# Rewriting the opening of a Fourier-mixing and gated feed-forward kernel: load queues, matrix phases, the DRAM round trip and the order of the other loads

## The chip, the cores and the metric

The kernel runs on one core of one Trainium2 chip. The metric is the device time of one execution in microseconds; the median of three runs is compared. A core has a matrix engine (TensorE, PE in the profile; PEld is its weight load), three engines for elementwise work (VectorE or DVE, ScalarE or ACT, GpSimd or POOL) and SyncE (SP), which here only issues transfers. SP, ACT and POOL each feed a transfer queue of their own: q1, q10 and q0 in the profile. The 16 DMA engines serve all three.

## The reference: what is computed

For x of shape (8, 3008, 256), in float32:

```python
X = np.fft.fft(np.fft.fft(x, axis=1), axis=2).real      # then rows (24064, 256)
g = X @ w_gate                                          # (256, 1536)
val = X @ w_val
gelu = 0.5 * g * (1.0 + erf(g / sqrt(2)))
out = (gelu * val) @ w_out                              # (1536, 256)
```

## The kernel before: how the work is staged

The sequence length is 3008 = 64 x 47. The Fourier transform over it is done as two matrix stages, and the transform over the 256 channels is folded into the weights.

**Opening.** For batch 0, `load_x` (L157) brings x(0) in three pieces of 8 slots; each piece is two transfers of 64 partitions (h = 0 to partitions 0 to 63, h = 1 to 64 to 127), all on SP's queue. `fold_x` (L172) adds and subtracts mirrored channels (L188, L189) and copies two columns (L190). The matrix G of the first stage is generated: `gen_g` (L246) multiplies and adds phases (L250, L253), reduces them (`reduce_phase`, L243 and L244) and takes a sine on ACT (L256). `a_step` (L396) multiplies G with the folded x, two slots a step, twelve steps a batch; the result is evacuated to S1 by DVE (L402) or ACT (L401) in turn. `z_write` (L405) stores S1 to a DRAM tensor z in two halves of four transfers each (L413, 32 partitions each), and `z_read` (L417, issue L423) reads it back to Ap in two transfers with another partition order: this is the round trip. Meanwhile `gen_t` (L261) and `gen_c` (L292) generate the other matrices, and `gen_w` (L306) casts the two weight matrices from float32 on POOL (L311), multiplies them with the channel matrix CW (L316) and evacuates the products to WE, WOP and WOM (L320 to L323). `load_w` (L209) loads these weights on ACT's queue, `load_wo` (L216, issue L220) the output weights on POOL's queue, casting them on the way; `load_x(1, i)` loads batch 1. `b_steps` (L425) is the second stage: for four q, an even and an odd half of 8 or 16 small matmuls (L442, L443, L448) on Ap, evacuated to Y by DVE (L463). `n_first` (L343) sends one row of Y through DRAM to all partitions (nrow, nq).

**Main loop.** 288 units follow, 36 a batch: three chunks of Y's columns by twelve blocks of the hidden width. A unit has five or six matmuls with 512 columns (`layer1`, L508), two Gelu on ACT (L529, L540), and the products on DVE (L544, L553, and for most units L519 and L558) and POOL (L567). The second layer of the chunk before (L592) is put between, 8 matmuls a unit. The first and second stage of the next batch are spread over the units: `a_step(b + 1, k)` in units 0 to 11 (for batch 1 two a unit, in units 6 to 11), `z_read` in units 12 and 13, `b_steps` later. Loads for batch b + 2 go out at units 0, 12 and 24, their folds on POOL from the fourth unit after.

**What sets the order.** A scheduler lays out each engine's instructions by their readiness in its own model. `keep_in_program_order` (`pin`, L151) ties an instruction behind the one traced before it on its engine. Before, this is on only in the main loop (`held`), and never for SP's transfers. `issue_after(ins)` ties what the block traces on the engine of `ins` behind `ins`: issue order on that engine, nothing else. Before, `load_w` is tied behind an evacuation on ACT, `load_wo` behind a cast on POOL, `load_x(1, i)` behind the last `z_read` on SP (L648). A tile from a pool with `bufs=3`, such as xin, waits until the work on the tile three before it is done.

Of the kernel before, what the change touches and what calls it, by code (L numbers as in the profile page):

```python
# [14 lines left out]
MAGIC = 12582912.0  # L15
TWO_PI = 2.0 * math.pi

# [11 lines left out]
def kernel(  # L29
# [20 lines left out]
    nc = tc.nc  # L50

# [40 lines left out]
    col_a = const_pool.tile([128, 1], FP32)  # L92
    col_b = const_pool.tile([128, 1], FP32)
# [51 lines left out]
    def z_tile():  # L145
        return dram.tile([2, NJ, NG, C], BF16, tag="z", bufs=2, name="z")


    held = [False]

    def pin(ins):  # L151
        return tc.keep_in_program_order(ins) if held[0] else ins
# [4 lines left out]
    def load_x(b, i):  # L157
# [3 lines left out]
        for h in range(2):  # L161
# [6 lines left out]
            nc.sync.dma_start(  # L168
# [3 lines left out]
    def fold_x(b, i, eng, a0=0, an=None):  # L172
# [7 lines left out]
        for (p0, pn, s0, sn) in parts:  # L180
# [7 lines left out]
            pin(eng.tensor_tensor(ea, lo, hi, op=ALU.add))  # L188
            pin(eng.tensor_tensor(od, lo, hi, op=ALU.subtract))  # L189
            pin(eng.tensor_copy(  # L190
# [5 lines left out]
    def iota(t, pattern, base, mult):  # L196
        nc.gpsimd.iota(t, pattern=pattern, base=base, channel_multiplier=mult,
                       allow_small_or_imprecise_dtypes=True)

    iota(col_p, [[0, 1]], 0, 1)  # L200
    iota(rowj, [[15, HJ]], 0, 0)
    iota(_sub(rowk, [[1, 33]], 0), [[1, 33]], 0, 0)
    iota(_sub(rowk, [[1, 31]], 33), [[1, 31]], 1, 0)
    for i in range(3):
        load_x(0, i)
# [3 lines left out]
    def load_w():  # L209
        for i, w_hbm in enumerate((moe_w_gate, moe_w_val)):  # L210
            t = work.tile([128, NCH, F], FP32, tag="h", bufs=2, name="wst")
            wst[i] = t
            src = ap_replace(w_hbm, ap=[[F, 128], [128 * F, NCH], [1, F]], offset=w_hbm.offset)
            nc.scalar.dma_start(out=_sub(t, [[F, NCH], [1, F]], 0), in_=src)

    def load_wo():  # L216
# [3 lines left out]
        nc.gpsimd.dma_start(out=_sub(Wo_sb, [[C, NFC], [1, C]], 0), in_=src)  # L220

    iota(_sub(rowc, [[1, 128]], 0), [[1, 128]], 0, 0)
    iota(_sub(rowc, [[1, 128]], 128), [[1, 128]], 0, 0)
# [5 lines left out]
    def scratch(n, name):  # L229
        return work.tile([128, n], FP32, tag="ev", bufs=3, name=name)  # L230

    xf_zero = [_sub(t, [[1, C]], (HJ - 1) * C, N1, N1) for t in xf_bufs]
    for t in xf_zero:
        nc.vector.memset(t, 0.0)
    nc.vector.memset(G, 0.0)
    nc.vector.memset(_sub(rowq, [[1, 33]], 0), 0.25)
    nc.vector.memset(_sub(rowq, [[1, 31]], 33), 0.0)
    nc.vector.tensor_scalar(col_a, col_p, 64.0, 296.0, op0=ALU.is_ge, op1=ALU.mult)
# [535 lines left out]
```

## Time and profile before

| what | us |
|---|---|
| median of 3 runs (672.79 to 678.3) | 674.6 |
| the profiled execution | 674.43 |
| its span, first to last instruction | 672.7 |
| PE busy, share of the span | 632.1, 94% |
| DVE, ACT, POOL busy | 540.3, 449.9, 460.3 |
| first matmul of stage one (L396) | 13.70 |
| first and second read of z landed (PE goes on) | 41.25 and 44.78 |
| first matmul of the main loop (L508) | 47.33 |
| first matmul of the second layer (L592) | 71.50 |

Times within the execution count from the span's start. A timeline line has start, duration, engine, line, operation, output and inputs, and in brackets the idle time before it and what ended it. A line of the chain has start, duration and the work on it. A line of the windows has each engine's busy time with its instruction count, then the granted clock of PE, the busy share of the DMA engines and their GB/s. A queue line has packets, megabytes, and the time of these packets as a share of 16 engines.

### The profile page before, as it was taken

To read this page: it belongs to the slowest core of one execution; us is meant where nothing else is said; L and a number is where in the kernel's file an instruction comes from. 1 tells how busy PE (TensorE), PEld (TensorE's weight loads), DVE (VectorE), ACT (ScalarE), POOL (GpSimd) and SP (SyncE) were. 2 spreads that over 40 slices of the span, in tenths; PEclk is the share of its full clock that TensorE was granted. 3 is DMA by queue.
4 is the path that set the end of the run, shared out by engine and by line. 5 is a ranking of instruction groups with operands and counts; after the bars stand their busy time and mean duration, and the time that the engine had idled before them with its cause. 6 is when DMAs were issued, how large, how long until landed. Compare 5 with 4: busy or idle time off the path is not lost.

```text
span 672.7 us, 13986 instructions
## 1 busy us (share of the span) xinstructions
PE 632.1 (94%) x4571; PEld 414.4 (62%) x4624; DVE 540.3 (80%) x896; ACT 449.9 (67%) x944; POOL 460.3 (68%) x726
## 2 busy tenths in 40 slices
PE   1389999998999999999999999999999999999997
PEld 0144666665666666666666666666666666666666
DVE  7947988696877978788886987778886998789981
ACT  2347667775777767776677776786777767666662
POOL 1409698886698886977788886977778444645450
PEclk9989999998999999999999999999999999999999
DMA  8898854557457465357453574266221463111113
GB/s 183 282 232 179 195 147 106 126 124 196 103 130 164 119 159 131 80 133 177 109 131 92 125 183 119 69 152 157 76 62 44 97 168 74 45 33 46 48 48 76
DMA packets 65577, 82.70 MB, mean 123 GB/s; under 512 B 8959, under 2 KB 59359, under 8 KB 61408
## 3 DMA queue, kind: packets, MB, share of 16 engines
q1 hardware_dynamic: 63408, 77.87, 48.1%
q10 hardware_dynamic: 544, 3.15, 1.4%
q0 software_dynamic: 1552, 0.79, 0.9%
q8 instruction: 36, 0.59, 0.4%
q14 instruction: 37, 0.30, 0.2%
HBM read 45.13 MB, written 37.44 MB: 123 GB/s over the span
## 4 chain that ended last, share of the span: by engine, by line
PE 87%; DMA 5%; DVE 5%; issue 1%; ACT 1%; SPq 0%; ACTq 0%; DVEq 0%
PE ps_o L592 36%; PE ps_g L508 25%; PE ps_v L508 19%; DMA Ap<-z 4%; PE ps_d L396 2%; PE ps_d L448 2%; DMA xin<-in_x_dram 1%; DVE h L544 1%; DVE h L553 1%; DVE xf L189 1%; DMA z<-S 0%; DVE S L402 0%; DVE ev L519 0%; DVE xf L188 0%; DVE sc L244 0%
## 5 line engine op out<-in xcount | busy, mean ns | idle before, releaser
L567 POOL TENSOR_TENSOR h<-gl,dv 128x512 bf16<-128x512 bf16 (+1 forms) x216 | 246.6, 1142 | 152.3 <-DVE dv L558 110.4
L592 PE MATMUL ps_o<-Wo_sb,h 128*128 128x256 bf16 (+2 forms) x2304 | 297.5, 273 | 0.0
L544 DVE TENSOR_TENSOR h<-gl,ps_v 128x512 bf16<-128x512 bf16 (+1 forms) x288 | 192.2, 677 | 99.3 <-ACT gl L540 77.1
L529 ACT ACTIVATE gl<-ps_g 128x512 bf16<-128x512 f32 (+1 forms) x288 | 169.4, 588 | 151.8 <-PE ps_g L508 110.2
L592 PEld LDWEIGHTS <-h 128*128 128x128 bf16 (+2 forms) x2304 | 227.4, 100 | 66.4 <-issue 2.5
L540 ACT ACTIVATE gl<-ps_g 128x512 bf16<-128x512 f32 (+1 forms) x288 | 168.7, 586 | 6.8 <-remote 6.3
L519 DVE SCALAR_TENSOR_TENSOR ev<-nq,WN,ps_v 128x512 f32<-128x512 bf16 (+1 forms) x216 | 157.6, 730 | 4.2 <-PE ps_v L508 2.7
L558 DVE SCALAR_TENSOR_TENSOR dv<-ev,ps_v 128x512 f32<-128x512 f32 (+1 forms) x216 | 144.2, 668 | 0.0
L508 PE MATMUL ps_v<-Y,WE 128*128 128x512 bf16 (+1 forms) x287 | 108.3, 378 | 1.0 <-DVE h L553 0.4
L508 PE MATMUL ps_g<-Y,WOM 128*128 128x512 bf16 (+1 forms) x288 | 108.0, 375 | 0.1
L508 PE MATMUL ps_g<-Y,WOP 128*128 128x512 bf16 (+1 forms) x281 | 105.5, 376 | 2.0
L508 PE MATMUL ps_v<-Y,WOP 128*128 128x512 bf16 (+1 forms) x281 | 105.7, 376 | 0.4
L508 PE MATMUL ps_g<-Y,WE 128*128 128x512 bf16 (+1 forms) x250 | 93.9, 376 | 0.0
L188 POOL TENSOR_TENSOR xf<-xin 128x127 bf16<-128x127 f32 (+3 forms) x148 | 72.4, 489 | 23.6 <-DMA xin<-in_x_dram 22.0
L508 PEld LDWEIGHTS <-WOP 128*128 128x128 bf16 x576 | 56.0, 97 | 48.5 <-issue 2.9
L189 POOL TENSOR_TENSOR xf<-xin 128x127 bf16<-128x127 f32 (+3 forms) x148 | 72.5, 490 | 0.0
L508 PEld LDWEIGHTS <-WE 128*128 128x128 bf16 x576 | 56.3, 98 | 26.0 <-issue 1.8
L603 ACT ACTIVATE osb<-ps_o 128x512 f32<-128x512 f32 x80 | 47.8, 597 | 26.6 <-PE ps_o L592 23.9
L448 PEld LDWEIGHTS <-Ap 96*128 96x128 bf16 (+1 forms) x527 | 40.5, 97 | 32.0 <-issue 7.0
L553 DVE TENSOR_TENSOR h<-gl,ps_v 128x512 bf16<-128x512 bf16 (+1 forms) x72 | 48.5, 673 | 2.5 <-PE ps_v L508 2.3
L401 ACT ACTIVATE S<-ps_d 128x512 bf16<-128x512 f32 x74 | 44.7, 604 | 1.3 <-PE ps_d L396 1.3
L508 PEld LDWEIGHTS <-WOM 128*128 128x128 bf16 x360 | 35.1, 97 | 16.9 <-issue 1.1
(103 smaller groups left out, 379.8 us busy)
## 6 DMA issues: line engine op xcount, KB each, us to landing
out_dram<-osb SPq DMA_DIRECT2D x360, 64.0 KB
xin<-in_x_dram SPq DMA_DIRECT2D x40, 512.0 KB
z<-S SPq DMA_DIRECT2D x64, 192.0 KB
Ap<-z SPq DMA_DIRECT2D x16, 768.0 KB
xin<-in_x_dram SPq DMA_DIRECT2D x8, 448.0 KB
ngr<-nrow SPq DMA_DIRECT2D x7, 388.0 KB
wst<-in_moe_w_gate_dram ACTq DMA_DIRECT2D x1, 1536.0 KB
wst<-in_moe_w_val_dram ACTq DMA_DIRECT2D x1, 1536.0 KB
```

What stands on the lines that cost most here:

```text
L188: pin(eng.tensor_tensor(ea, lo, hi, op=ALU.add))
L189: pin(eng.tensor_tensor(od, lo, hi, op=ALU.subtract))
L448: pin(nc.tensor.matmul(ps[r, o : o + N2], w, t[:, s : s + N2], start=True, stop=True))
L508: pin(nc.tensor.matmul(ps[:, :n], W[:, i, r["fs"]], r["Y"][:, eo, r["c0"] : r["c0"] + n], start=start, stop=True, skip_group_check=not start))
L519: pin(nc.vector.scalar_tensor_tensor(r["ev"][:, :nm], r["nq"][:, r["c0"] : r["c0"] + nm], WN[:, fc : fc + 1], r["pv"][:, :nm], op0=ALU.mul ...
L529: pin(nc.scalar.activation(r["glm"][:, : r["nm"]], r["pg"][:, : r["nm"]], AF.Gelu))
L540: pin(nc.scalar.activation(r["glp"][:, :n], r["pg"][:, :n], AF.Gelu))
L544: pin(nc.vector.tensor_tensor(r["h"][:, r["fc"], :n], r["glp"][:, :n], r["pv"][:, :n], op=ALU.mult))
L553: pin(nc.vector.tensor_tensor(hm, r["glm"][:, :nm], pv[:, :nm], op=ALU.mult))
L558: pin(nc.vector.scalar_tensor_tensor(dv[:, :nm], r["ev"][:, :nm], 2.0, pv[:, :nm], op0=ALU.mult, op1=ALU.subtract))
L567: pin(nc.gpsimd.tensor_tensor(hm, r["glm"][:, :nm], r["dv"][:, :nm], op=ALU.mult))
L592: pin(nc.tensor.matmul(ps[:M, s * C : (s + 1) * C], h[:, fc, sign * 512 + sub * 128 : sign * 512 + sub * 128 + M], Wo_sb[:, fc, :], start= ...
```

## The change: what it does

- Every engine's instructions are tied in program order from the start (`_InOrder`); `pin` and `held` go. On SP only the transfers of batch 0 are tied (`sync`); the others keep `nc.sync`.
- x(0) goes out with h = 0 on SP's queue and h = 1 on ACT's.
- The phases of G (rowj x rowk + rowq) are computed on POOL, three times two operations of 128x512; DVE keeps the reduction. The offsets of rowj come from the iotas.
- `gen_c`'s DVE part goes ahead of `gen_g`; its sines (`sin_c`) come after the last `a_step`. `gen_t` is rewritten for the new partition order, its sines (`sin_t`) lie between parts of `gen_w`.
- z becomes [24, 128, 256], slot by slot. `z_write` is one transfer of 128 partitions; batch 0 writes three pieces of 8 slots and reads slots 0 to 15 (64 partitions of Ap) after the second piece and slots 16 to 23 (32 partitions) after the third. Later batches write two pieces and read as before.
- Pieces of 8 slots: fold of x(0) on DVE, with the last 2 or 3 slots of the second and third piece on POOL; four `a_step`, eight of the twelve evacuations on ACT only.
- The weights come in three column blocks of 512, the first behind x(0) on ACT's queue, the others after the first and second `z_write`; `gen_w` runs by block. The casts become [128, 2, 512].
- `load_x(1, i)` stands after the second stage, under `issue_after` of its first matmul (on PE). x(1)'s fold leaves the opening: 12 parts of two slots in units 1 to 8, on POOL and DVE in turn, at the end of a unit. `load_wo` goes to unit 1, `gen_tw` to unit 13; x(2)'s first load to unit 4.
- Batch 0's second stage takes four PSUM tags instead of two, its odd halves are evacuated on ACT, and a Gelu ahead of it brings the activation table in.

The diff, cut to its core:

```diff
+class _InOrder:
+    def __init__(self, tc, engine):
+        self._tc, self._engine = tc, engine
+
+    def __getattr__(self, name):
+        call = getattr(self._engine, name)
+        return lambda *a, **k: self._tc.keep_in_program_order(call(*a, **k))
...
+    sync, vec, act, pool, pe = (
+        _InOrder(tc, e) for e in (nc.sync, nc.vector, nc.scalar, nc.gpsimd, nc.tensor))
...
-        return dram.tile([2, NJ, NG, C], BF16, tag="z", bufs=2, name="z")
-
-
-    held = [False]
-
-    def pin(ins):
-        return tc.keep_in_program_order(ins) if held[0] else ins
+        return dram.tile([HJ, 128, C], BF16, tag="z", bufs=2, name="z")
...
-            nc.sync.dma_start(
+            eng = act if h and b == 0 else sync if b == 0 else nc.sync
+            eng.dma_start(
...
+    for i in range(3):
+        load_x(0, i)
+    for h in range(2):
+        iota(_sub(rowj, [[1, HJ]], 0, h * N1, N1), [[15, HJ]], 360 * h, 1)
     iota(col_p, [[0, 1]], 0, 1)
...
+    pool.tensor_scalar(rowk, rowk, 1.0 / 64.0, None, op0=ALU.mult)
+    pool.memset(_sub(rowq, [[1, 33]], 0), 0.25)
+    pool.memset(_sub(rowq, [[1, 31]], 33), 0.0)
...
-    def load_w():
+    def load_w(f0):
         for i, w_hbm in enumerate((moe_w_gate, moe_w_val)):
-            t = work.tile([128, NCH, F], FP32, tag="h", bufs=2, name="wst")
-            wst[i] = t
-            src = ap_replace(w_hbm, ap=[[F, 128], [128 * F, NCH], [1, F]], offset=w_hbm.offset)
-            nc.scalar.dma_start(out=_sub(t, [[F, NCH], [1, F]], 0), in_=src)
+            if i not in wst:
+                wst[i] = work.tile([128, NCH, F], FP32, tag="h", bufs=2, name="wst")
+            src = ap_replace(
+                w_hbm, ap=[[F, 128], [128 * F, NCH], [1, 512]], offset=w_hbm.offset + f0)
+            act.dma_start(out=_sub(wst[i], [[F, NCH], [1, 512]], f0), in_=src)
...
+    load_w(0)
+
+    def scratch(n, name):
+        return work.tile([128, n], FP32, tag="ev", bufs=3, name=name)
+
+    PH = []
+    for j0 in range(0, HJ, 8):
+        ph = scratch(512, "sa")
+        PH.append(ph)
+        v = _sub(ph, [[64, 8], [1, 64]], 0)
+        pool.tensor_tensor(
+            v, _sub(rowj, [[1, 8], [0, 64]], j0), _sub(rowk, [[0, 8], [1, 64]], 0), op=ALU.mult)
+        pool.tensor_tensor(v, v, _sub(rowq, [[0, 8], [1, 64]], 0), op=ALU.add)
...
+    vec.memset(xf_zero[0], 0.0)
+    vec.memset(G, 0.0)
+
+    def reduce_phase(ph, tmp):
+        vec.tensor_scalar(tmp, ph, MAGIC, None, op0=ALU.add)
+        vec.scalar_tensor_tensor(tmp, tmp, MAGIC, ph, op0=ALU.subtract, op1=ALU.subtract)
...
+    def gen_g(i):
+        red = red_tile()
+        reduce_phase(PH[i][:, :], red[:, :])
...
+        reds = []
         for t in range(NCH):
-            nc.vector.tensor_scalar(col_c, col_p, 128.0 * t, 1.0 / C, op0=ALU.add, op1=ALU.mult)
-            ph, tmp, red = scratch(512, "sa"), scratch(512, "sb"), scratch(512, "sc")
-            f = lambda u: u[:, :C]
-            nc.vector.scalar_tensor_tensor(f(ph), rowc, col_c, quac, op0=ALU.mult, op1=ALU.add)
-            reduce_phase(f(ph), f(tmp), f(red))
-            nc.scalar.activation(
-                _sub(CW, [[1, C]], t * C), f(red), AF.Sin, scale=-TWO_PI)
-
-
-    def gen_w():
-        nc.vector.tensor_scalar(col_m, col_p, 1.0, -2.0, op0=ALU.is_ge, op1=ALU.mult)
+            vec.tensor_scalar(col_c, col_p, 128.0 * t, 1.0 / C, op0=ALU.add, op1=ALU.mult)
+            both = red2_tile()
+            ph, red = both[:, :C], both[:, C : 2 * C]
+            vec.scalar_tensor_tensor(ph, rowc, col_c, quac, op0=ALU.mult, op1=ALU.add)
+            reduce_phase(ph, red)
+            reds.append(red)
+        vec.tensor_scalar(col_m, col_p, 1.0, -2.0, op0=ALU.is_ge, op1=ALU.mult)
+        return reds
...
+    def sin_c(reds):
+        for t in range(NCH):
+            act.activation(_sub(CW, [[1, C]], t * C), reds[t], AF.Sin, scale=-TWO_PI)
+
+    wbs = []
...
+            pool.tensor_copy(wb[:, :, fs], wst[i][:, :, fs])
...
-        if k % 2 or b > 1:
-            return pin(nc.scalar.activation(dst, ps, AF.Copy))
-        return pin(nc.vector.tensor_copy(dst, ps))
+        if b > 1 or (k % 2 if b else k < 8 or k % 2):
+            return (act.activation(dst, ps, AF.Copy))
+        return (vec.tensor_copy(dst, ps))
...
+        dst = ap_replace(
+            z[0:1, 0, :], ap=[[C, 128], [128 * C, nj], [1, C]], offset=z[j0, 0:1, :].offset)
+        (nc.sync if b else sync).dma_start(out=dst, in_=_sub(S1, [[C, nj], [1, C]], j0 * C))
...
+    def z_read(b, g0, ng, j0=0, nj=HJ):
         if "Ap" not in st[b]:
             st[b]["Ap"] = Ap_tile()
         z, Ap = st[b]["z"], st[b]["Ap"]
         src = ap_replace(
-            z[0, 0, 0:1, :], ap=[[NG * C, 2 * NJ], [1, ng * C]], offset=z[0, 0, g0 : g0 + 1, :].offset)
-        return nc.sync.dma_start(out=_sub(Ap, [[1, ng * C]], g0 * C), in_=src)
+            z[0:1, 0, :], ap=[[NG * C, 4 * nj], [1, ng * C]], offset=z[j0, g0 : g0 + 1, :].offset)
+        (nc.sync if b else sync).dma_start(
+            out=_sub(Ap, [[1, ng * C]], g0 * C, 4 * j0, 4 * nj), in_=src)
...
-                    box["ps"] = ps_o() if b == 0 and eo else ps_d()
+                    box["ps"] = ((ps_v, ps_o)[q % 2] if eo else (ps_d, ps_g)[q % 2])() \
+                        if b == 0 else ps_d()
...
-                if b:
-                    pin(nc.scalar.activation(o, i, AF.Copy))
+                if b or eo:
+                    (act.activation(o, i, AF.Copy))
                 else:
-                    nc.vector.tensor_copy(o, i)
+                    (vec.tensor_copy(o, i))
...
-    gen_g(0, 8)
-    fold_x(0, 0, nc.vector)
-    gen_g(8, 8)
-    fold_x(0, 1, nc.vector)
-    gen_g(16, 8)
-    fold_x(0, 2, nc.vector)
-    for k in range(12):
-        evac = a_step(0, k)
-        if k == 1:
-            with tc.issue_after(evac.ins):
-                load_w()
-        if k % 6 == 5:
-            z_write(0, 2 * (k - 5), 12)
-    gen_t()
-    gen_c()
-    with tc.issue_after(st[0]["mm"].ins):
-        gen_w()
-    with tc.issue_after(wst["last"].ins):
-        load_wo()
-    for i in range(2):
-        last_read = z_read(0, 16 * i, 16)
-    with tc.issue_after(last_read.ins):
-        for i in range(3):
-            load_x(1, i)
+    reds = gen_c()
     for i in range(3):
-        fold_x(1, i, nc.gpsimd)
-    gen_tw()
+        gen_g(i)
+        nd = (8, 6, 5)[i]
+        fold_x(0, i, vec, 0, nd)
+        if nd < 8:
+            fold_x(0, i, pool, nd, 8 - nd)
+        for k in range(4 * i, 4 * i + 4):
+            a_step(0, k)
+        z_write(0, 8 * i, 8)
+        if i < 2:
+            load_w(512 * (i + 1))
+        if i == 1:
+            z_read(0, 0, NG, 0, 16)
+    z_read(0, 0, NG, 16, 8)
+    sin_c(reds)
+    phase_t = gen_t()
+    vec.memset(xf_zero[1], 0.0)
+    gen_w(0)
+    sin_t(*phase_t)
+    gen_w(512)
+    gen_w(1024)
+    gen_wn()
+    act.activation(col_f[:, :], col_p[:, :], AF.Gelu)
     for q in range(4):
         for eo in range(2):
             steps, evac = b_steps(0, eo, q)
@@ -658,6 +687,9 @@
                 s()
             evac()
     n_first(0)
+    with tc.issue_after(st[0]["bmm"].ins):
+        for i in range(3):
+            load_x(1, i)
...
-            if i % 12 == 0 and b + 2 < B:
+            if i in ((0, 12, 24) if b else (4, 12, 24)) and b + 2 < B:
...
-            if i % 12 >= 4 and b + 2 < B:
-                fold_x(b + 2, i // 12, nc.gpsimd, i % 12 - 4, 1)
+            if b == 0:
+                for k in {1: (0, 1), 2: (2,), 3: (3, 4), 4: (5,), 5: (6, 7), 6: (8,),
+                          7: (9, 10), 8: (11,)}.get(i, ()):
+                    fold_x(1, k // 4, (pool, vec)[k % 2], k % 4 * 2, 2)
+                if i == 1:
+                    load_wo()
+                if i == 13:
+                    gen_tw()
+            f, fp = i % 12 - 4, i // 12
+            if b == 0 and i < 16:
+                f, fp = i - 8, 0
+            if f >= 0 and b + 2 < B:
+                fold_x(b + 2, fp, pool, f, 1)
```

## The prediction, made before the changed kernel ran

> **What bounds the kernel now.** I read the page first: its head and the forty slices of PE.
>
> ```profile
> span 672.7 us, 13986 instructions
> PE 632.1 (94%) x4571; PEld 414.4 (62%) x4624; DVE 540.3 (80%) x896; ACT 449.9 (67%) x944; POOL 460.3 (68%) x726
> PE   1389999998999999999999999999999999999997
> ```
>
> PE is the bound from the third slice on; the first three (50 us) are the opening. The change can win back at most what PE idles there, and what the first units lose. So I read, next, the chain of waits between 20 and 50 us.
>
> ```profile
> 29.46 3.19 DMA z<-S
> 33.11 11.63 DMA Ap<-z
> 44.78 0.37 PE ps_d L448 x8
> ...
> 47.33 1.10 PE ps_v L508 x2
> ```
>
> The round trip ends last: 11.63 us of reading z, then 2.55 us to the first unit. Why the read is slow is told by the queues and the windows.
>
> ```profile
> q0 software_dynamic: 939, 0.48, 91.9%
> q1 hardware_dynamic: 55, 0.45, 35.4%
> ...
> 4.00:6.00 2.00, 0.00 (x0) 0.00 (x0) 0.73 (x2) 0.00 (x0) 0.00 (x0) 1.00 1.04 238
> 18.00:20.00 2.00, 1.28 (x7) 0.61 (x4) 2.00 (x7) 0.00 (x0) 0.00 (x0) 1.00 0.93 369
> ```
>
> From 34 to 38 us the output weights (q0) hold the engines and the read (q1) moves 0.45 MB. From 42 to 46 both queues move 136 packets: one packet each in turn, large or small. A load into 64 partitions runs at 221 to 238 GB/s (x(0), 4 to 6 us), one into 128 at 369 (weights, 18 to 20 us). The last view is DVE beside POOL in the timeline.
>
> ```profile
> 26.86 0.48 DVE L300 SCALAR_TENSOR_TENSOR sa<-rowc,col_c,quac 128x256 f32<-128x256 f32 x1
> 28.09 3.22 POOL L311 CAST wb<-wst 128x1536 bf16<-128x1536 f32 x2 [2.81 <-DMA wst<-in_moe_w_val_dram]
> 28.41 1.57 DVE L244 SCALAR_TENSOR_TENSOR sc<-sb,sa 128x256 f32<-128x256 f32 x1
> 30.01 1.57 DVE L300 SCALAR_TENSOR_TENSOR sa<-rowc,col_c,quac 128x256 f32<-128x256 f32 x1
> ```
>
> The same L300 takes 0.48 us alone and 1.57 beside a cast on POOL: each of the two operations ends just after a cast does. The engines take turns, one operation each, where DVE reads only SBUF. In the main loop DVE reads PSUM and this doesn't show.
>
> **The change part by part.** The sum is made against the profiled execution, 674.43 us (span 672.7 and 1.7 around it), 0.2 below the median of 674.6.
>
> *First fold.* DVE: memsets to 2.84 as now and 0.35; `gen_c` two times 0.48 + 0.28 + 0.45 and 0.4 of small ones; reduction 0.42 + 0.68; fold 1.21 + 1.14 + 0.2. In all 3.2 + 6.4 = 9.6 us if nothing blocks. POOL: seven iotas of 0.13, 0.4 of small ones, then six operations of 512 float32. POOL's fold rows (1016 in 2.34 us) give 1.17 each, 7.0 in all, from 2.2 us. These lie exactly beside `gen_c`. If they alternate with DVE, DVE gets all 7.0 on top, less the 1 us before it arrives, and about 1.4 of POOL's part of the next fold: 17.0. The ends are 9.6 and 17.0; the near row is the pair at 28.41 and 30.01, so I take 17.0. Now this fold ends at 11.6 and the first matmul starts at 13.70. That row shows a cast on POOL, not an operation with two inputs. The Trainium skill (SBUF — State Buffer, two separate sides) says that a VectorE operation with two SBUF inputs and any GpSimd operation that reads SBUF exclude each other for the whole instruction. By that rule 17.0 stands; by its opposite 9.6 would.
>
> *x(0) on two queues.* Six issues of 0.68 on SP become three, and three of 0.43 on ACT. At 229 GB/s piece 0 is there at 8.2 us as now, at 369 about 6.3. With the fold waiting for the reduction until 13.4, both cost nothing. The skill's same page (Can I just issue two DMAs to hit both halves?) says that it is no use, +6%; in the sum that changes nothing, in the fast rival below 1 to 2 us.
>
> *To the last evacuation.* Four steps a piece, evacuated on ACT, 0.53 apart: 17.0 + 0.5 + 2.2 = 19.7. Then ACT issues two weight loads (0.9), runs two sines (1.3) and four evacuations: 24.6. The third fold on DVE has four casts on POOL beside it (1024 at 0.95 ns, 1.0 each) and ends at 28.4; last evacuation 31.0, or 29.0 without the casts. Now 25.5.
>
> *Round trip.* The write of piece 1 goes out at 24.7 against 2.1 MB of weights on the other queue, packet by packet: landed between 27.5 (alone) and 31.7 (weights first). Then SP issues the read of 16 slots: 1.05 MB into 64 partitions at 229 is 4.6 us, with issue and landing 34.5 to 38.6. The third write is queued behind that read on SP and in the ring: 0.52 MB at 310 (z writes now, 26 to 30 us), 36.2 to 40.3. The last read, 0.52 MB at 229: 40.6 to 45.0. Now 44.78. So taking the output weights away is worth about 4 us here, and the later S1 and the added order give it back.
>
> *Weight products.* They begin after `sin_c`, 31.9. 24 matmuls at 0.43 as now (0.22 after some 8 us of work, as at 38.5 now), then 0.8: 41.7. They don't end after the latest read, but nearly.
>
> *Second stage.* All four q lie behind the last read; now half are done by then. Two q take 2.10 us now (44.78 to 46.88); with four PSUM tags I take 0.85 each, with 0.7 for the last evacuation 4.1. First unit: 44.7 to 49.1. The weight products and the reads both point to the upper half; I take 48.0, against 47.33: **+0.7**.
>
> *First units.* x(1)'s fold was POOL's alone (15 us from 49.9, waited for by nobody). Now DVE takes six parts of two slots: the line through 1016 in 1.21 and 127 in 0.27 gives 0.41, twice, and 0.15: 0.97 each, 5.8 in all. Behind it on DVE stand the products of the next unit, for which PE waits two units later. DVE's idle time from 52 to 64 us is 2.1, with the half-clocked stretch from 48 on 5.3. So +0.4 to +3.7; beside POOL's own parts (0.6 an operation) up to 3.5 more; if x(1) isn't there at unit 1, up to 4 more. Queued straight after the last read, its first MB lands at 44.1 + 4.6 + 0.9 = 49.6, before unit 1 ends, so I leave the last two out: **+3.5**.
>
> *Rest.* The output weights, 1536 packets, need 6.5 us alone (235 a us, 34 to 38 us now). They are wanted 24 us after the first unit: covered, unless q1 is full all that time (34 packets a us): up to +3. The write of z for later batches is two issues instead of eight; PE waits for these reads 3.1 us in all:
>
> ```profile
> PE ps_d L442 <- DMA Ap<-z: 3.1, 2, 2.2
> ```
>
> With the slower stretch behind the longer wait 0 to 3.5 us could go; late there is SP's queue more than the write, so **-1**. Program order on all engines is what the main loop had already: 0. The Gelu table (1.28 us) now comes under the last read: 0, or 1.3 if the read is early.
>
> Sum: 674.4 + 0.7 + 3.5 - 1.0 = 677.6, say 678, no change that a measurement of this kernel (about 1%) can tell. Its own range, by the ends above, is 669 to 687.
>
> **The rivals.**
>
> *A, the opening really gets short (faster).* If DVE isn't blocked on POOL, the fold ends at 9.6, the last evacuation at 21.6, the last read lands between 33 and 37.4, weight products at 32.4, first unit at 37 to 41.6, middle 39.3: -8. With the folds in DVE's idle time (+0.4) and -1: 666. For it: x(0) could be twice as fast; the iotas, seen so far, block nobody. Against it: the row of 1.57.
>
> *B, x(1) isn't held (slower).* `issue_after` names a matmul on PE and x(1)'s loads are SP's, so nothing ties them. That SP's loads pass earlier ones is seen:
>
> ```profile
> 54.79 0.47 SPq L168 DMA_DIRECT2D xin<-in_x_dram  x1
> 58.10 0.36 SPq L346 DMA_DIRECT2D nq<-nrow  x1
> ```
>
> The load for batch 2 stands after nq in the program and before it in the queue. Each half piece (0.52 MB) in front of the round trip costs 2.3 us at 229 GB/s. One or two fit into the ring's pauses before the second write. From the third on the first unit moves: three +4, all six +10, of which the wait for x(1) gives 2 back. 678 + 8 = 686. Against it: the load of x(2) at unit 12 (75.03 us) wasn't drawn ahead although its tile was free at about 60.
>
> *C, the output weights late.* q1 full with x(1), x(2) and z until unit 12: +3 on the forecast, 681.
>
> **How the numbers follow.** Chances: forecast 0.42, A 0.30, B 0.20, C 0.08. Faster by over 1% (below 667.9): 0.24 of A and 0.02 of the forecast, 0.26. Slower by over 1% (above 681.3): B's 0.20, 0.09 of the forecast, 0.03 of C: 0.32. Within 1%: 0.42. The range leaves out A's lower end (a first unit before 37) and B with C together: 662 to 688.
>
> **What would show it.** Right: DVE operations of `gen_c` at 1 us and more beside POOL's phases, the first L396 near 17 us, the last read landing at 41 to 45, the first L508 near 48, DVE without idle time in units 1 to 8. Wrong in A's way: `gen_c` at 0.3 to 0.5 us each, first L508 before 42. Wrong in B's way: loads of x(1) between the writes of z on SP's queue, the last read after 48. Wrong in size: a first unit as forecast, but the first L592 more than 30 us after it.

## The result and the profile after

The changed kernel takes 692.97 us (median of four, 690.98 to 698.29), the kernel before 674.86 in the same comparison (672.79 to 678.3): a ratio of 1.0275, 95% interval 1.0204 to 1.0347. It is slower by 18 us, and 693 lies outside the predicted 662 to 688. The profiled execution took 693.31 us, its span is 691.5, 18.8 more than before. Three stretches of PE's work divide that difference:

| stretch | before | after | forecast | measured |
|---|---|---|---|---|
| start to the first matmul of the main loop | 47.3 | 56.9 | +0.7 | +9.5 |
| first 12 units, to the first matmul of the second layer | 24.2 | 26.5 | +3.5 | +2.3 |
| the rest, to the end of the span | 601.2 | 608.2 | -1.0 | +7.0 |

Helpers record nearly every instruction now, so in the profile after nearly all lines are L25 (`_InOrder`), and one reads by tiles. Only SP's untied transfers keep their own: L176 is `load_x`, L443 the z write and L451 the z read of later batches, L604 a store. The head of the page and PE's slices come first; PE and its granted clock are two rows of the same forty slices of 17.3 us.

```profile
span 691.5 us, 13974 instructions
PE   1609899998999989999999999999999999999997
PEclk9957999999999999999999999999999999999999
```

PE's third digit is 0 where it was 8: from 35 to 52 us PE does next to nothing, and its clock falls to 0.5. The windows of the changed kernel (busy time with instruction counts for PE, PEld, DVE, ACT and POOL; clock, DMA share, GB/s):

```profile
40.00:50.00 10.00, 0.00 (x0) 0.00 (x0) 0.00 (x0) 0.00 (x0) 0.00 (x0) 0.50 1.14 221
```

From 40 to 50 us no engine does anything; the DMA engines alone are full. What they carry is told by SP's queue (start, time, engine, line, operation; issues only):

```profile
15.01 1.11 SPq L176 DMA_DIRECT2D xin<-in_x_dram  x2
17.75 0.41 SPq L25 DMA_DIRECT2D z<-S  x1
18.98 0.47 SPq L176 DMA_DIRECT2D xin<-in_x_dram  x1
21.94 0.37 SPq L25 DMA_DIRECT2D z<-S  x1
23.13 1.14 SPq L176 DMA_DIRECT2D xin<-in_x_dram  x1
33.33 0.45 SPq L25 DMA_DIRECT2D Ap<-z  x1
33.89 0.53 SPq L25 DMA_DIRECT2D z<-S  x1
34.47 0.84 SPq L176 DMA_DIRECT2D xin<-in_x_dram  x1
```

The three L176 lines up to 23.13 are four transfers of x(1), four half pieces ahead of the first read of z. The code puts x(1) under `issue_after` of a matmul on PE, and on SP that ties nothing. The first read is issued at 33.33, 11.4 us after the second write, whose landing it waits for. The third write has a half piece of x(1) behind it and a neighbour on POOL's queue. The chain's longest piece puts a price on it (start, time, work), and the queues from 41 to 45 us name the neighbour (packets, MB, share):

```profile
33.89 13.21 DMA z<-S
```

```profile
q0 software_dynamic: 821, 0.42, 75.7%
q1 hardware_dynamic: 818, 0.41, 51.9%
```

q0 is the load of the output weights. POOL, which waits for nothing of x(1) since x(1) is already there, ran ahead to unit 1 of its own program and issued it at 32.42 (31.25 before). So neither of the "other loads" is held back. q0 and q1 move a packet each in turn, and the third write takes 13.2 us.

For the rest of the span, the waits of PE for z:

```profile
PE ps_d L25 <- DMA Ap<-z: 8.0, 4, 3.1
```

3.1 us in two waits before, 8.0 in four now. The first of them, in SP's queue of the changed kernel:

```profile
159.19 0.47 SPq L176 DMA_DIRECT2D xin<-in_x_dram  x1
159.76 0.53 SPq L443 DMA_DIRECT2D z<-S  x1
167.13 0.79 SPq L451 DMA_DIRECT2D Ap<-z  x2
```

A half piece of x stands ahead of the second z write of the batch. It waits for a buffer that POOL's fold frees at 159.2; the write waits behind it on SP, and then behind its 0.5 MB on the engines. By the count of transfers it is the first half of x(4): x(3) ended with its piece of 448 KB at 138.75. In the program it stands 25 units later, so the scheduler drew it ahead by most of a batch. The same stands ahead of the second write in the next three batches (240.76, 321.59 and 399.89), and these are the four waits. Before, the half piece that lay here (the second piece of x(3)) stood behind the write, though still ahead of the reads:

```profile
146.81 2.41 SPq L413 DMA_DIRECT2D z<-S  x4
152.95 0.47 SPq L168 DMA_DIRECT2D xin<-in_x_dram  x1
153.59 0.93 SPq L423 DMA_DIRECT2D Ap<-z  x2
```

### The profile page after: what moved, and what is told of

Its sections match the earlier page's. It is cut to its first block, busy times and chain, and to the rows that moved or that the text cites. A ratio compares the mean times of both kernels' runs of the same rounds, so it can differ in the third digit from the quotient of the medians.

```text
span 691.5 us, 13974 instructions
## 1 busy us (share of the span) xinstructions
PE 633.2 (92%) x4571; PEld 415.2 (60%) x4624; DVE 546.8 (79%) x892; ACT 454.7 (66%) x959; POOL 472.6 (68%) x753
## 4 chain that ended last, share of the span: by engine, by line
PE 83%; DMA 7%; DVE 7%; issue 1%; ACT 1%; ACTq 0%; DVEq 0%; SPq 0%
PE ps_o L25 35%; PE ps_g L25 24%; PE ps_v L25 18%; PE ps_d L25 5%; DMA Ap<-z 4%; DMA z<-S 3%; DVE xf L25 2%; DVE h L25 2%; DVE red L25 2%; ACT gl L25 0%; DVE S L25 0%; DVE ev L25 0%; DVE G L25 0%; DVE quat L25 0%; ACT WE L25 0%
## 5 line engine op out<-in xcount | busy, mean ns | idle before, releaser
L25 ACT ACTIVATE gl<-ps_g 128x512 bf16<-128x512 f32 (+1 forms) x576 | 309.5, 587 | 160.7 <-PE ps_g L25 116.8
L25 POOL TENSOR_TENSOR h<-gl,dv 128x512 bf16<-128x512 bf16 (+1 forms) x216 | 246.7, 1143 | 166.8 <-DVE dv L25 120.3
L25 DVE TENSOR_TENSOR h<-gl,ps_v 128x512 bf16<-128x512 bf16 (+2 forms) x360 | 237.3, 676 | 105.0 <-ACT gl L25 81.7
L25 PE MATMUL ps_o<-Wo_sb,h 128*128 128x256 bf16 (+2 forms) x2304 | 298.2, 273 | 0.0
L25 PEld LDWEIGHTS <-h 128*128 128x128 bf16 (+2 forms) x2304 | 227.7, 100 | 66.8 <-issue 2.8
L25 POOL TENSOR_TENSOR xf<-xin 128x127 bf16<-128x127 f32 (+2 forms) x306 | 139.6, 477 | 34.3 <-DMA xin<-in_x_dram 34.3
L25 DVE SCALAR_TENSOR_TENSOR ev<-nq,WN,ps_v 128x512 f32<-128x512 bf16 (+1 forms) x216 | 157.6, 729 | 5.9 <-PE ps_v L25 4.2
L25 DVE SCALAR_TENSOR_TENSOR dv<-ev,ps_v 128x512 f32<-128x512 f32 (+1 forms) x216 | 144.2, 667 | 0.0
L25 PE MATMUL ps_v<-Y,WE 128*128 128x512 bf16 (+1 forms) x287 | 108.4, 378 | 0.9 <-DVE h L25 0.7
L25 PE MATMUL ps_g<-Y,WOM 128*128 128x512 bf16 (+1 forms) x288 | 108.2, 376 | 0.1
L25 PE MATMUL ps_g<-Y,WOP 128*128 128x512 bf16 (+1 forms) x281 | 105.5, 376 | 2.0
L25 PE MATMUL ps_v<-Y,WOP 128*128 128x512 bf16 (+1 forms) x281 | 105.6, 376 | 0.5 <-issue 0.2
L25 PE MATMUL ps_g<-Y,WE 128*128 128x512 bf16 (+1 forms) x250 | 94.1, 376 | 0.0
L25 PEld LDWEIGHTS <-WOP 128*128 128x128 bf16 x576 | 56.1, 97 | 48.7 <-issue 3.1
L25 PEld LDWEIGHTS <-Ap 96*128 96x128 bf16 (+1 forms) x568 | 43.8, 100 | 61.9 <-issue 28.7
L25 ACT ACTIVATE osb<-ps_o 128x512 f32<-128x512 f32 (+2 forms) x112 | 58.3, 535 | 32.9 <-PE ps_o L25 29.6
L25 PEld LDWEIGHTS <-WE 128*128 128x128 bf16 x576 | 56.3, 98 | 26.1 <-issue 2.3
L25 ACT ACTIVATE S<-ps_d 128x512 bf16<-128x512 f32 x74 | 44.7, 604 | 2.5 <-PE ps_d L25 2.5
L25 PEld LDWEIGHTS <-G 128*128 128x128 bf16 x192 | 19.5, 102 | 44.4 <-ACT G L25 18.5
L25 PEld LDWEIGHTS <-WOM 128*128 128x128 bf16 x360 | 35.1, 97 | 16.8 <-issue 0.8
L25 ACT ACTIVATE Y<-ps_d 128x192 bf16<-128x192 f32 (+4 forms) x140 | 36.7, 348 | 0.0
L25 POOL CAST xf<-xin 128x2 bf16<-128x2 f32 (+1 forms) x153 | 31.3, 205 | 0.0
```

The costliest lines, as they stand in the source:

```text
L25: return lambda *a, **k: self._tc.keep_in_program_order(call(*a, **k))
```

## The experiments

All times are medians. Each run was compared with the kernel before, measured beside it: 674.9 us for "after" (the changed kernel), 674.8 for e1 to e4, 674.7 for e5, e7, e8 and e11, 673.9 for e9, e10, e12 and e14. In brackets is the 95% interval of the ratio; runs of different groups are best compared by their ratios. The last three columns are stretches of the one profiled execution, as in the table above. In e2, e4 and e14 that execution was the slowest of its run: 695.04, 687.15 and 668.35 us.

| run | us | ratio | to the main loop | 12 units | rest |
|---|---|---|---|---|---|
| before | 674.8 | 1 | 47.3 | 24.2 | 601.2 |
| after | 692.97 | 1.0275 [1.0204, 1.0347] | 56.9 | 26.5 | 608.2 |
| e1_hold_x | 683.61 | 1.013 [1.0099, 1.0161] | 47.9 | 26.3 | 607.1 |
| e2_hold_wo | 693.01 | 1.0273 [1.0235, 1.031] | 52.6 | 34.8 | 605.9 |
| e3_split | 686.12 | 1.0179 [1.0126, 1.0231] | 57.8 | 26.6 | 598.5 |
| e4_tie | 682.55 | 1.0109 [1.0076, 1.0142] | 58.5 | 30.5 | 596.4 |
| e5_hold_tie | 672.3 | 0.997 [0.995, 0.999] | 47.3 | 27.3 | 596.3 |
| e7_pool_fold | 668.62 | 0.9921 [0.9894, 0.9949] | 47.4 | 23.6 | 596.3 |
| e8_ph_dve | 665.96 | 0.9878 [0.9839, 0.9917] | 43.5 | 23.5 | 596.3 |
| e9_one_q | 669.21 | 0.9922 [0.9893, 0.9951] | 47.4 | 23.9 | 596.3 |
| e10_w_late | 670.4 | 0.9943 [0.9923, 0.9963] | 48.0 | 24.1 | 596.3 |
| e11_write3_first | 666.45 | 0.9892 [0.9845, 0.9938] | 44.9 | 23.5 | 596.3 |
| e12_ph_w3 | 668.33 | 0.9908 [0.9877, 0.994] | 46.6 | 23.9 | 596.3 |
| e14_g2_early | 666.5 | 0.9885 [0.9851, 0.992] | 46.5 | 23.8 | 596.3 |

**e1_hold_x: batch 1's x behind the last read of z, on SP.**

```diff
-    with tc.issue_after(st[0]["bmm"].ins):
+    with tc.issue_after(last_read.ins):     # last_read = z_read(0, 0, NG, 16, 8)
```

> The changed kernel with one edit: x(1)'s loads are tied behind the last read of z on SP's queue (as they were before), so none is ahead of the round trip. GpSimd's stream then also waits for x(1) before it reaches the load of the output weights, so that load moves back too. Theory Q (the unheld loads make the opening late: three x(1) halves ahead of the second write, then a half and the output weights beside the third): the first read goes out near 25 us instead of 33.3, the last one lands near 37 instead of 52.2, first main-loop matmul near 42 instead of 56.9, time 678 to 682. Rival L (VectorE and GpSimd in turns and the later S1 make it late): the first main-loop matmul stays above 52 and the time above 688.

Measured: 683.61 us, 9.4 less; in the profile 9.0 us of it are in the opening (56.9 to 47.9). SP's queue of this run:

```profile
17.19 4.69 SPq L25 DMA_DIRECT2D z<-S  x2
29.09 0.46 SPq L25 DMA_DIRECT2D Ap<-z  x1
29.66 0.53 SPq L25 DMA_DIRECT2D z<-S  x1
38.34 0.34 SPq L25 DMA_DIRECT2D Ap<-z  x1
```

The output weights went with it, to 49.62 us: POOL's first fold of x(1) stands ahead of them in its program. So this run shows x(1) and the output weights together. The expected 42 us for the first unit was not reached: the second write still needs 7.6 us to land (about 21.5 to 29.1), though nothing of x(1) is near (e10 tells why), and the third 8.7, behind the megabyte of the first read on its own queue (e11).

**e2_hold_wo: output weights alone held, until GpSimd has copied a cell of Y.**

```diff
                 if i == 1:
+                    pool.tensor_copy(gate_t, _sub(Ys[0], [[1, 1]], YW + 24))
                     load_wo()
```

> The changed kernel with one edit: one GpSimd copy of an element of Y ahead of the load of the output weights, so that this load really waits for the second stage; x(1)'s loads stay as they are. Theory Q: the third write no longer shares the engines packet by packet with 1536 packets; it lands some 5 us sooner (42 instead of 47), first main-loop matmul near 52, time near 688. If the output weights don't matter, nothing moves by more than 1 us. The copy itself is 0.2 us.

Measured: the opening is 4.3 us shorter and the first units 8.3 us longer, so that nothing is won. The opening is as expected: the third write lands in 8.5 us instead of 13.2, with x(1) where it was. On SP's queue:

```profile
34.34 0.53 SPq L25 DMA_DIRECT2D z<-S  x1
42.82 0.34 SPq L25 DMA_DIRECT2D Ap<-z  x1
```

The time is not. POOL stands at the copy until 53, then does its folds of x(1) back to back beside VectorE's. In this run's timeline of DVE, the first of these folds and a later one of the same shape (two operations each):

```profile
57.90 4.37 DVE L25 TENSOR_TENSOR xf<-xin 128x254 bf16<-128x254 f32 x2
64.65 0.74 DVE L25 TENSOR_TENSOR xf<-xin 128x254 bf16<-128x254 f32 x2
```

4.37 us beside POOL's folds, 0.74 without. The products h queue behind it, and PE waits for them:

```profile
62.99 0.59 PE L25 MATMUL ps_v<-Y,WOM 128*128 128x512 bf16 x1 [3.72 <-DVE h L25]
```

The forecast's *First units* had named this ("beside POOL's own parts (0.6 an operation) up to 3.5 more") and left it out. In the changed kernel GpSimd's folds are done early and it does not show; in e2 it takes all that was won.

**e3_split and e4_tie: the later batches.** e3 writes z as four transfers of 32 partitions again for later batches; the order on SP goes back by itself. e4 leaves one transfer and ties the load of the third piece of x(b+2) behind the second z read.

```diff
# e3
-        (nc.sync if b else sync).dma_start(out=dst, in_=_sub(S1, [[C, nj], [1, C]], j0 * C))
+        for p in range(0, 128, 32):          # b > 0
+            nc.sync.dma_start(out=part, in_=_sub(S1, [[C, nj], [1, C]], j0 * C, p, 32))
# e4
+                if i == 24:
+                    with tc.issue_after(st[b + 1]["zr"].ins):
+                        load_x(b + 2, 2)
```

> The changed kernel with one edit: for batches 1 to 7 each write of z is four transfers of 32 partitions again instead of one of 128; the layout stays. In the queue that comes out, the half of x that stood ahead of the second write in the changed kernel stands behind it again. Theory O (the place of that half is what makes the reads late): waits of TensorE for z in the main loop fall from 8.0 us to about 3, time down by about 6, to 687. Theory S (one transfer of 128 partitions lands later by itself): the same here, but not with the write left whole (next run).

> The changed kernel with one edit: the third piece of x for the batch after next is tied behind the second read of z on SP's queue; the write of z stays one transfer. The opening is as in the changed kernel. Theory O: waits of TensorE for z in the main loop fall from 8.0 to 1 to 3 us, time near 686 to 688. Theory S: the waits stay above 6 us and the time within 2 us of the changed kernel's 693.

Measured: both heal the rest, 608.2 to 598.5 and to 596.4. In e4 PE waits nowhere for z in the main loop, with one transfer a write. So it is not the form of the write that costs, but the place of the x half on SP's queue; the form only changed where the scheduler put it. SP's queue in e4, at the same batch:

```profile
164.40 0.38 SPq L443 DMA_DIRECT2D z<-S  x1
168.81 1.31 SPq L451 DMA_DIRECT2D Ap<-z  x2
```

The reads follow the write after 4.4 us instead of 7.4. No load of x lies between: the tied piece, x(3)'s third, goes out at 178.88, and x(4) comes behind it. In e4's profile the first units take 30.5 us, and PE's longest wait there is 4.1 us for h, behind VectorE's last folds of x(1), where a cast of 0.17 us takes 1.70 beside GpSimd, as in e2. (The median is 4.6 us below this execution, so the others need not have had all of that wait.)

**e5_hold_tie: both.**

> Two edits at once on the changed kernel: batch 1's x tied behind batch 0's last read on SyncE, and the load of the third piece of x(b+2) tied behind the second z read of its batch. Alone they measured 683.61 and 682.55 us against 692.97, so 9.4 and 10.4 us. Theory O, two separate causes (the opening's queue, and the place of one x half in every later batch): the gains add, 692.97-9.4-10.4 = 673.2 us, say 672 to 676, and PE's waits for z in the main loop are under 1 us. Rival: both edits heal the same stretch, and the sum stays at 680 or above.

Measured: 672.3 us. The two gains add (673.2 by the sum), and the whole loss of the change is accounted for. The rest is 596.3 us, 4.9 below the kernel before: that has two waits for z, 3.1 us, and behind the longer one the granted clock is down (0.91 from 160 to 180 us), which is another 1.8. The longer wait is the one with the half piece of x ahead of the reads; the cause of the other, of 0.9 us, is open.

**e7_pool_fold: x(1)'s folds on GpSimd alone, output weights behind them.**

```diff
-                    fold_x(1, k // 4, (pool, vec)[k % 2], k % 4 * 2, 2)
-                if i == 1:
+                    fold_x(1, k // 4, pool, k % 4 * 2, 2)
+                if i == 6:
                     load_wo()
```

> On top of the two ties: all twelve fold chunks of batch 1 on GpSimd (every second one was on VectorE), and the load of the output weights placed in GpSimd's own order at unit 6, behind the fold that waits for x(1)'s third piece. Theory: VectorE's folds, in program order ahead of the products h, hold the first 12 units (26.3 to 26.6 us in the runs so far, 24.2 before): they come back to 24 to 25 us and the time is 2 us under that of the run with the two ties alone. Rival: GpSimd alone is late with the folds, first-stage matmuls of batch 1 wait from unit 6 on, and the time is equal or up to 2 us above.

Measured: 668.62 us, the first units 23.6 us. PE's waits for h in the units go from 2.4 to 0.6 us, and nobody waits for the folds. Two edits went in together, so the 3.7 us are theirs together.

**e8_ph_dve: the phases of G on VectorE again.** In `gen_g`, `vec.tensor_tensor` twice a third, in place of `pool.tensor_tensor`; otherwise e7.

> As the run with all folds on GpSimd, but the six phase operations of the first-stage matrix are VectorE's again (one product and one addition for each third, 0.68 us each before), in gen_g. Theory L (VectorE and GpSimd take turns): gen_c's six wide operations, 0.99 to 1.44 us beside GpSimd's, come down to 0.3 to 0.5 us, so the first fold starts at 9 to 9.5 us instead of 11.44 although VectorE does 1.4 us more; the last first-stage evacuation 1 to 2 us earlier, and the first units up to 2 us earlier. Rival: the slow operations are VectorE's own, and the first fold starts later, at 12.5 or after. By both the time moves by 2 us at most, since the DMA round trip follows.

Measured: 665.96 us, a little more than the 2 us of either theory; the main loop begins at 43.5 us instead of 47.4. DVE's timeline of the changed kernel, of e7 (later operations) and of this run:

```profile
3.04 0.99 DVE L25 SCALAR_TENSOR_TENSOR red<-rowc,col_c,quac 128x256 f32<-128x256 f32 x1
...
11.44 2.89 DVE L25 TENSOR_TENSOR xf<-xin 128x1016 bf16<-128x1016 f32 x2
```

```profile
19.12 5.43 DVE L25 SCALAR_TENSOR_TENSOR red<-red,sa 128x512 f32<-128x512 f32 x1
24.47 1.53 DVE L25 TENSOR_TENSOR xf<-xin 128x635 bf16<-128x635 f32 x2
```

```profile
3.04 0.49 DVE L25 SCALAR_TENSOR_TENSOR red<-rowc,col_c,quac 128x256 f32<-128x256 f32 x1
...
8.35 2.34 DVE L25 TENSOR_TENSOR xf<-xin 128x1016 bf16<-128x1016 f32 x2
...
18.79 5.42 DVE L25 SCALAR_TENSOR_TENSOR red<-red,sa 128x512 f32<-128x512 f32 x1
24.13 3.22 DVE L25 TENSOR_TENSOR xf<-xin 128x635 bf16<-128x635 f32 x2
```

Theory L holds for the first fold, which starts 3.1 us sooner although DVE does more. It fails for the end of stage one: the last evacuation is 1.3 us later than in e7 (29.4 against 28.1). The operation of 5.42 us is not the difference, since e7 has it too; the third fold is, with 3.22 us against 1.53, beside two more casts on POOL. The long operation lies beside these on POOL, in the same run:

```profile
19.69 3.97 POOL L25 CAST wb<-wst 128x1024 bf16<-128x1024 f32 x4
```

The gain came all the same, by another way than expected: the second write goes out about 2.5 us sooner and lands sooner (first read at 26.50 instead of 28.82), and the third write, issued 3.5 us behind the first read instead of 0.6 (at 30.02), lands in 5.1 us instead of 8.5 (in e7 it has that read's megabyte ahead of it).

**e11_write3_first: both reads of z behind the third write (on e7).**

```diff
-        if i == 1:
-            z_read(0, 0, NG, 0, 16)
+    z_read(0, 0, NG, 0, 16)
     last_read = z_read(0, 0, NG, 16, 8)
```

> As the run with all folds on GpSimd, but both z reads of batch 0 behind the third z write, so that the write does not stand behind a read that waits for the second write's landing. In the run with x(1) held the third write was issued at 29.66 us, behind read A at 29.09, and read B at 38.34. Theory: the third write goes out 3 us earlier (about 26.5), read B 2 to 3 us earlier, the first matmul of the main loop 2 to 3 us earlier, and the time follows. Rival: the weights share the transfer engines until 35 us, the two writes only share what there is, and read B moves by under 1 us.

Measured: 666.45 us, the main loop 2.5 us sooner. SP's queue of e7, and of this run:

```profile
28.82 0.46 SPq L25 DMA_DIRECT2D Ap<-z  x1
29.38 0.53 SPq L25 DMA_DIRECT2D z<-S  x1
37.90 0.34 SPq L25 DMA_DIRECT2D Ap<-z  x1
```

```profile
28.64 0.36 SPq L25 DMA_DIRECT2D z<-S  x1
29.10 0.53 SPq L25 DMA_DIRECT2D Ap<-z  x1
32.49 0.34 SPq L25 DMA_DIRECT2D Ap<-z  x1
```

The theory holds in the end, not in its first step: the third write goes out only 0.7 us sooner (28.64, where 26.5 was expected), since the last evacuation ends at about 28.6. But with no read ahead of it, it lands in 3.9 us, and the last read goes out at 32.5 instead of 37.9.

**e9_one_q: x(0) on SP's queue alone (on e7).** `eng = sync if b == 0 else nc.sync`.

> As the run with all folds on GpSimd (668.62 us), but x(0)'s six half pieces all on SyncE's queue, as before the change. Theory T (the two queues share the same transfer engines, busy all the while from 3 us on): x(0)'s third piece lands at most 1.5 us later than the 15.9 to 16.6 us at which GpSimd's fold could start, the last first-stage evacuation at most 1 us later, the time up to 1 us higher or the same. Rival: a queue on its own reaches only part of the memory's rate; the third piece lands 4 us later or more and the time rises by 2 us or more.

Measured: 669.21 us, as e7. The DMA engines are full by either way: in the windows of two microseconds from 4 to 14 us they move 206 to 254 GB/s with one queue and 213 to 262 with two (means 233 and 244). The third piece comes 4 us later with one queue (21.0 us against 16.6), which is the rival's number, but not for its reason. On ACT's queue the first load of the weights is issued at 0.74 us in e9 and at 3.00 in e7.

With one queue for x(0) nothing stands ahead of the weights on ACT's, so they go out at once and share the engines with x(0). What the second queue does for x(0) is to keep the weights behind it. The time did not feel it: stage one ended even earlier in e9 (last evacuation at 25.6 us against 28.1), as GpSimd's casts of the weights came after VectorE's folds there.

**e10_w_late: second and third part of the gate and value weights behind the last evacuation (on e7).**

```diff
-        if i < 2:
-            load_w(512 * (i + 1))
+        if i == 2:
+            load_w(512)
+            load_w(1024)
```

> As the run with all folds on GpSimd, but the second and third part of the gate and value weights are issued by ScalarE behind the last Sin of the first-stage matrix and the last evacuations (about 28 us; 16.4 and 20.7 now), behind z write 2. Theory W (weights on the other queue, packet by packet, slow the z writes): write 2, issued about 21.5, lands in 4 to 5 us instead of 7, so that read A goes out at 25.5 to 26.5 instead of 28.82; the weight products then end at 42 to 44 instead of 37, and since TensorE has them ahead of the second stage the first unit starts no earlier, and up to 2 us later: time +0 to +3 us. Rival: the write's 512 byte pieces set its time, read A stays at 28 to 29 and the first units start 3 us later or more.

Measured: 670.4 us, within theory W's 0 to +3 (by the ratios 1.5 us above e7, with intervals that overlap). SP's queue of this run:

```profile
24.75 0.46 SPq L25 DMA_DIRECT2D Ap<-z  x1
26.67 0.36 SPq L25 DMA_DIRECT2D z<-S  x1
39.23 0.34 SPq L25 DMA_DIRECT2D Ap<-z  x1
```

Without weights beside it the second write lands in 3.3 us (21.5 to 24.75) instead of 7.4. The third, behind the first read on its own queue and beside both weight loads, takes 12.6 instead of 8.5. A write of z is as slow as what shares the engines with it, and moving the weights moves the loss.

**e12_ph_w3 and e14_g2_early: the two single gains together; and with `gen_g` of the third piece ahead of DVE's second fold.**

> The run with all folds on GpSimd, with both single edits that made it faster: the matrix phases on VectorE (668.62 to 665.96) and the third z write ahead of the reads (668.62 to 666.45). Theory: TensorE's weight products, which end at 39 to 40 us with the phases on VectorE (there the second stage waits 0.9 us for WNb and not for a read), are the next limit, so the gains do not add: 665.0 to 666.0 us. Rival: they add, 668.62-2.66-2.17 = 663.8 us.

> As the run with both edits, and gen_g of the third piece ahead of VectorE's second fold. In the run with the phases on VectorE one of its operations of 0.69 us took 5.42 us from 18.79 on, beside four copies of GpSimd (wb from wst, 3.97 us back to back from 19.69 on), and the third fold started at 24.13. Theory: GpSimd's copies kept VectorE out; with that operation out of their way the third fold starts at 19 to 21 us, the last first-stage evacuation at 24 to 26 instead of 29.4, the weight products end 3 to 4 us earlier, and the time is 2 to 4 us under that of the run with both edits. Rival: the next VectorE operation takes the same delay in its place (the fold itself, two operands of 4 bytes), and the time is equal within 1 us.

Measured: 668.33 and 666.5 us. The gains of e8 and e11 do not even hold together: in e12's profile the main loop begins at 46.6 us, later than in either (43.5 and 44.9); the intervals of the three ratios overlap. The reason given was wrong too: PE waits 3.7 us for a read, not for the weight products. In e8 the third write comes late (30.02), and with the reads put behind it, the first read goes out at 30.53 instead of 26.50. Whether to wait depends on which of the two is ready first. e14 takes the long operation away; its theory holds for stage one (third fold at 20.19 instead of 24.15, last evacuation near 27 instead of 30), and the median is 1.8 us less than e12's, just under the 2 to 4 expected; the two reads of z, 12 us from the first issue to the second stage, end last there (PE waits 5.6 us for them). That profile is of an execution no faster than e12's, so what won the 1.8 us is not seen in it. Of all versions e8, e14 and e11 are the fastest, 1.2, 1.15 and 1.1% below the kernel before; between these three the intervals tell nothing.

## Why the prediction was wrong, step by step

**x(1) is held: failed, the step that decided the opening.** The *Round trip* had the last read land at 40.6 to 45.0; it landed at 52.03. Its sum had only weights beside the writes. The rival B described what happened, loads of x(1) between the writes and a last read after 48. Its 8 us on a first unit at 48.0 make 56.0, and it was 56.9, but that is luck: B's price is for x(1) alone, and the output weights had a share in the loss that B didn't count. With these held (e2) the main loop begins at 52.6, and with x(1) held as well (e1) at 47.9: 4.3 us for the output weights, and then 4.7 for x(1). What was wrong is B's chance of 0.20. The text on record said itself that the tie names a matmul on PE and ties nothing on SP; against that it set one load in the main loop that had not been drawn ahead. One load that stays is weak evidence beside one that is seen to pass. Together the two are 9.0 us of the 9.5.

**The output weights are held: failed.** They were counted late (rival C, +3). They were early, since nothing in POOL's own program waited once x(1) was there. The *Round trip*'s "about 4 us" for taking them away was near e2's 4.3, but they stayed.

**Rest, -1: failed, by 8 us.** The text saw that "late there is SP's queue more than the write", and took the write's shorter issue as a small gain. It did not ask what the scheduler, which lays SP's untied transfers out by readiness, would do with the x half once the write was a single instruction. e3 and e4 show it: 608.2 goes to 598.5 or 596.4 with the x half behind. What a wait costs PE is more than the wait: the granted clock stays at half afterwards. The windows of the changed kernel behind a wait of 3.08 us that ends at 173.98 (clock third from the end):

```profile
174.00:176.00 2.00, 2.00 (x10) 0.90 (x11) 0.00 (x0) 0.94 (x2) 1.48 (x5) 0.50 0.91 276
176.00:178.00 2.00, 2.00 (x16) 1.33 (x14) 0.83 (x2) 0.26 (x1) 0.00 (x0) 0.67 0.36 79
```

The clock is full again from about 177.3 on (0.67 over these two microseconds, 1.00 in the next), so 3.3 us went at half speed and 1.7 us of work are lost on top of 3.1. The four waits are 3.1, 2.3, 1.4 and 1.2 us. The clock falls behind the first two alone: it is 0.91 from 160 to 180 and from 240 to 260 us, and 1.00 in every such window between and behind them up to 680. So 8.0 us of waits and twice 1.7 make 11.4 of the 11.8 us between 608.2 and 596.4. The Trainium skill (TensorE: Matmul & The Clock Gate, What's actually happening) puts both steps of the clock at about 3.4 us, of idling on the way down and of work on the way up. The windows agree on the way up. On the way down they don't: a wait of 2.3 us was enough, and there the clock fell at about 255.8, 1 us after PE had gone on. Behind the long wait of the opening they don't agree on the way up either: PE works from 52.2 us on, and the clock is at 0.50 until 61 and at 1.00 from 62, so some 9 us.

**First fold, 17.0: right in kind, too dear.** `gen_c`'s six wide operations took 7.1 us instead of some 2.4 (0.99 to 1.44 each), as the row of 1.57 and the Trainium skill (SBUF — State Buffer, two separate sides) said; e8, with POOL out of the way, gives 0.29 to 0.49. But the fold ended at 15.0: POOL took 4.7 us from `gen_c` and about 1 from the fold, not 6.0 and 1.4. (By the same terms the fold would have had its reduction at 13.1, not 13.4; nothing hangs on it.) The last evacuation, forecast for 31.0, came at about 26. So stage one ended 5 us sooner than forecast, and the main loop began 9 us later all the same: what failed lies in the transfers.

**x(0) on two queues costs nothing and wins nothing: right.** The skill's same page (Can I just issue two DMAs to hit both halves?) has +6% for it; e9 against e7 gives 233 and 244 GB/s, 5%, but in e9 the weights go beside x(0) on the other queue. The kernel before has SP's queue alone: 238, 229 and 229 GB/s in the three windows from 4 to 10 us, against 242, 213 and 262 in e7, 3%.

**Weight products, 41.7; second stage, 4.1: one early, one about right.** The products ended at about 35.5 and covered nothing after that; the second stage took 4.7 us at half clock.

**First units, +3.5: +2.3 measured,** from VectorE's folds, as far as e7 tells: without them (and with the output weights later) the units go from 27.3 to 23.6.

## What to carry to other kernels

An issue-order tie holds only what is issued on the engine of the instruction that it names: before counting a load as held, ask on which queue it stands, what in that queue it waits for, and if nothing, put it at the time when its buffer comes free. On a queue without such ties an edit to one transfer can move its neighbours, and a load that waits for a buffer ahead of a write that is ready costs the write, its read and, behind that, TensorE's clock. And a gain that depends on order (e8, e11) must be measured in the version it goes into: together the two began the main loop later than each alone.

## What the runs showed of the hardware that was not expected

VectorE and GpSimd do not always take turns one operation each. One VectorE operation of 0.69 us took 5.42 beside four casts of GpSimd that ran back to back for 3.97 us (e8; 5.43 in e7), and ended 0.55 us behind the last of them; two fold operations of 0.74 us together took 4.37 beside GpSimd's folds (e2): the forecast had counted one operation of the other engine for each of its own. When GpSimd gives way and when it doesn't was not found out.

Two queues can move one packet each in turn, whatever these hold: 821 and 818 packets in 4 us in the changed kernel (0.42 and 0.41 MB), 136 and 136 in 4 us before (0.07 and 0.86 MB, from 42 to 46 us). But they don't always. In e7 the first write of z was issued at 17.20, and from 19 to 21 us only the weights' queue moved packets:

```profile
q10 hardware_dynamic: 305, 0.59, 96.7%
```

The write's packets came from 21 us on; why they had to wait is open. The same write of 0.5 MB landed in 3.3 us with nothing beside it (e10, second write), in about 7.4 beside the weights, and behind that first write (e7, second), 8.5 behind a read of 1 MB on its own queue (e7, third), and 13.2 behind that read, beside the output weights (the changed kernel, third).
